# Weight pieces and two first layers kept in order, state products on the mix's PSUM buffers, a sorting copy moved

## The chip, the cores and the metric

The kernel runs on one core of a Trainium2 chip. The metric is the device time of one execution in microseconds; less is better. The core has five engines with a queue of instructions each: PE (matrix products, into the eight banks of PSUM), DVE and ACT (element-wise work, and all reading of PSUM), POOL (element-wise work in SBUF and indirect DMAs) and SP (here only DMA issues). Every engine works through its own queue in order and waits on semaphores for the others.

## What is computed

A block-wise linear attention with decay, then a Fourier mixing block with a two-layer network:

```python
for b in range(nb):                      # attention, blocks of 64 rows
    intra = einsum('bhic,bhjc->bhij', qb, kb) * Dmask
    intra = einsum('bhij,bhjd->bhid', intra, vb)
    inter = einsum('bhid,bhde->bhie', qb * lam_pow, kv_state)
    out[:, :, sl] = intra + inter
    kv_state = lam_block * kv_state + einsum('bhsd,bhse->bhde', kb * rev_pow, vb)
x = out as (B, S, H*D)
u = x + real(fft(fft(x, axis=1), axis=2))
un = (u - mean(u)) / sqrt(var(u) + 1e-6)
return u + maximum(un @ w_ch1, 0) @ w_ch2
```

Batch 4, 8 heads of 64, 768 rows, width 512, hidden width 2048. All products are in f32. The two weight matrices come as f64 and are turned into f32 on the chip with bit operations.

## The kernel before

**Attention** (`attention`, line 526) is a generator of twelve steps: four batches, three steps each, 256 rows a step. It yields an estimate of time at three places of a step, and a planner mixes other work in there. In step i: `turn_k` and `turn_q` transpose the next step's k and q on PE into PSUM, and ACT copies them out (L391 to L398); DVE multiplies q by its powers of the decay, `qpow` (L400). `sort` (L380) is a POOL copy of k for the step after that, which waits for the load of k. `back` transposes the outputs of the step before into rows (L467; DVE L490 and L491 or ACT L474 to L478 copy them out). `to_state` multiplies k and v (L406) into PSUM; DVE adds the product to the state (L414, L416), and POOL makes the next decayed state (`decayed`, L421). `within` makes the outputs (L447). Then the loads of later steps are issued on SP (L367, L371). `begin` makes the scores (L426, DVE L432 multiplies by the decays), scales k on POOL (L386) and adds the state's part (L441).

**PSUM.** While `strict[0]` holds, tiles are taken from eight fixed banks by hand: `psum_t` goes round banks 0 to 3 (transposes, scores, state products), `psum_o` round 4 and 5, and `psum_a` round 6 and 7 (everything of the mix). Later, tiles come from two pools of five and three buffers.

**The mix** (`fft_ln`, line 698) of one batch: DVE folds the rows (L597 to L691), PE makes five products with the Fourier tables (L724, ACT L728), then three wide products (L736 to L741, DVE L816 to L831), statistics on DVE (L755, L756) and POOL (L759, L760), and for three pairs of row tiles a norm (`norm`: DVE L776, and where the first network takes them PE transposes L783 and ACT L787). For batch 0 the last two norms are not run there but put into `held`, and the network's generator calls them later.

**Weights** (`weights`, line 274): 32 pieces of 128x512. The first sixteen are the first half of both matrices. Each is fetched (`fetch`) and converted (`convert`): DVE L261, ACT L262, DVE L263, L266, L269, L270, one unit of the planner's time. While `strict[0]` holds, the fetch goes through ACT's queue into buffers of the network, up to two pieces ahead; later through SP's queue into the three `words` buffers, which attention also uses for k and q.

**The network** (`mlp`, line 871): for 256 rows a first layer (L878, ACT L886 or DVE L884) and a second layer (L892). Each product in f32 stands in the trace as two matmul records, so half a first layer (eight column blocks of four products) is 64 records of L878.

**Order.** `P(i)` keeps an instruction in program order among all that are kept, as long as `strict[0]` holds; `keep` does so always. Everything else is placed by the scheduler of the language, which may put it ahead of kept instructions on the same engine. The driver (lines 1516 to 1542) writes the mixing out: `mixed((gen, t), ...)` advances that generator which has used the smallest share of its t; `run` exhausts one. It starts with attention alone, mixes in weight pieces until the first batch's rows are there, then the mix of batch 0, attention and pieces in four stages, then what is left of attention, then pieces until eight have landed. There `strict[0]` ends. The first layers of the first two networks follow beside pieces, and then the rest: network halves beside the mixes of batches 1 to 3 and the remaining pieces. From L1160 on come the last row tiles with a seven-product scheme, which the change does not touch.

Of the kernel before, what the change touches and what calls it, by code (L numbers as in the profile page):

```python
# [11 lines left out]
F32 = mybir.dt.float32  # L12
# [65 lines left out]
def kernel(  # L78
# [69 lines left out]
    def P(i):  # L148
        return keep(i) if strict[0] else i
# [5 lines left out]
    banks = [new(pa, [128, 512], "pa") for _ in range(5)] + [new(pm, [128, 512], "pm") for _ in range(3)]  # L155
    turn = {"s": 0, "m": 0, "o": 0}

    def held_bank(i, shape):
        t = banks[i]
        if len(shape) == 2:  # L160
            return t[:, 0:shape[1]]
        return t[:, 0:shape[1] * shape[2]].rearrange("p (a b) -> p a b", a=shape[1])
# [9 lines left out]
    def psum_a(shape):  # L172
        if strict[0]:
            turn["m"] += 1
            return held_bank(6 + turn["m"] % 2, shape)
        return new(pa, shape, "pa")
# [15 lines left out]
    for hd in HD:  # L192
        P(nc.vector.tensor_copy(pulse[hd, 1:C + 1:2], ident[hd, hd]))
    decay = const.tile([128, H, C + 1], F32, name="decay")
    for h in [*range(0, H, 2), *range(1, H, 2)]:
        P(scan(decay[:, h, :], lamb[:, h:h + 1].broadcast_to([128, C + 1]), pulse, 0.0, op0=ALU.mult, op1=ALU.add))

    lamq = const.tile([128, HP], F32, name="lamq")
# [4 lines left out]
    for m in [1 << e for e in range(7)]:  # L203
        P(nc.vector.tensor_tensor(qpow[:, :, m:2 * m], qpow[:, :, 0:m], qpow[:, :, m - 1:m].broadcast_to([128, HP, m]), op=ALU.mult))
    spow = qpow[:, :, C - 1:C]

# [23 lines left out]
    def load_tables(i):  # L230
        if i == 1:
            P(nc.sync.dma_start(cs, cn["cs"].ap()))
            P(nc.sync.dma_start(ix, cn["ix"].ap()))
        elif i == 2:
            P(nc.sync.dma_start(dt, cn["dt"].ap()))
# [5 lines left out]
    def fetch(j, src):  # L241

        if strict[0]:
            raw = hp_.tile([128, 2 * WP], U32, tag="hr", name=f"raw{j}")
        else:
            raw = words[j % 3].bitcast(U32)
        if strict[0]:
            P(nc.scalar.dma_start(raw, src.bitcast(U32)))
        else:
            P(nc.sync.dma_start(raw, src.bitcast(U32)))  # L250
        return raw
# [150 lines left out]
    def to_state(i):  # L402
        n, vt, kd = i % SC, v_of[i % 2], k_of[i % 2]
        chunks = (0, 1) if n < SC - 1 else (0,)
        pu = [psum_t([128, HP, D]) for _ in chunks]
        lead(P(mm(pu[ch][HD[hi], hp, :], lhsT=kd[HD[ch], 2 * hp + hi, r, :], rhs=vt[HD[ch], 2 * hp + hi, r, :],  # L406
# [119 lines left out]
    def attention():  # L526
# [26 lines left out]
        for i in range(n):  # L553
            yield 1.5
            if i + 1 < n:
                turn_k(i + 1)
                if i + 2 < n:
                    sort(i + 2)
                turn_q(i + 1)
            yield 2.5  # L560
            if i:
                back(i - 1)
            if i + 1 < n:
                to_state(i + 1)
            within(i)
            if i + 2 < n:
                load(i + 2, "v")
            if i + 3 < n:
                load(i + 3, "kq")
            if i in TABLES:  # L570
                load_tables(TABLES[i])
            yield 5.0
            if i + 1 < n:
                begin(i + 1)
# [8 lines left out]
    odd = const.tile([128, HM], F32, name="bs")  # L583
    for t in ys + [odd]:
        P(nc.gpsimd.memset(t, 0.0))

# [111 lines left out]
    def fft_ln(b):  # L698
# [104 lines left out]
        def wide(t):  # L803
            ps = psum_a([128, DM])
            width(t, ps, False, keep if (b, t) == PLAIN[1] else lambda i: i)
            A = halves(ps)[:, ::-1, 0:QM]
# [6 lines left out]
        def summed(t, ds, A):  # L813
            if strict[0]:
                yield 0.6
            P(nc.vector.tensor_tensor(even_odd(ds[:, 0:HM]), A, even_odd(odd[:, :]), op=ALU.subtract))  # L816
            P(nc.vector.tensor_tensor(even_odd(ds[:, HM + 1:2 * HM + 1]), A, even_odd(odd[:, :]), op=ALU.add))
            u, v_ = xs[b, t], xs[b, HC + t]
            if strict[0]:
# [29 lines left out]
        if b in LEADS:  # L849
            two, none = norm(2), norm(0)  # L850
            held.update({(b, 1, 1): two, (b, 1, 4): two, (b, 1, 7): none, (b, 1, FO): none})
            return
# [626 lines left out]
    def run(gen):  # L1479
        return sum(gen)  # L1480
# [37 lines left out]
    run(part(att, 9.0))  # L1518
    run(mixed((until(att, lambda: (0, 0) in xs), 20.0), (w, 4.0)))
    run(mixed((mix, T_FOLD), (att, 3.6 * t_step)))  # L1520
    run(mixed((mix, 8.0), (att, 0.9 * t_step), (w, 2.5)))
    run(mixed((mix, 22.0), (att, 3.0 * t_step), (w, 1.0)))
    run(mix)
# [5 lines left out]
    lead_half = chain(half[0])  # L1529
    run(mixed((att, 1.3 * t_step), (w, 1.5)))  # L1530
    run(att)
    run(until(w, lambda: landed[0] >= 8))
    strict[0] = False
    run(mixed((part(lead_half, 13.5), 13.6), (w, 2.0)))
    run(mixed((part(half[0][1], 13.5), 13.6), (w, NW / 2 - landed[0])))
    run(until(w, lambda: landed[0] >= NW // 2))
    run(mixed((lead_half, t_half - 27.0), (fr, 62.0), (w, 0.5 * NW)))
    run(w)
# [49 lines left out]
```

## Time and profile before

| | us |
|---|---|
| median of 3 runs | 792.33 |
| lowest, highest | 791.04, 792.41 |
| the profiled execution | 791.95 |
| its span, first to last instruction | 790.1 |
| PE busy | 748.2 (95%) |
| DVE busy | 612.6 (78%) |
| ACT busy | 200.5 (25%) |
| POOL busy | 184.7 (23%) |

A row of a timeline has the start, the busy time, engine, line, operation, what is written from what, the shape and the count; in brackets stands the idle time of the engine just before it and who ended it. A row of the groups has the busy time and the mean of one in ns, then the idle time before them. Times are from the span's start. A PE that is busy need not be at its peak, and the granted clock is given as a share of full speed.

### The profile page before, as it was taken

What the parts mean: (1) busy time and instruction counts of PE and PEld (TensorE: products, weight loads), DVE (VectorE), ACT (ScalarE), POOL (GpSimd) and SP (SyncE); (2) the same over time, 40 slices, a digit from 0 to 9 for tenths busy, and PEclk for the clock granted to TensorE, in tenths of its full rate; (3) what the DMA queues carried; (4) which work ended last, traced back from release to release, by engine and by line L of the source; (5) the groups of instructions that cost most, each with busy time, mean ns of one, the idle gap of its engine ahead of it and who ended that gap; (6) DMA issues with size and microseconds to landing.
All of it is one profiled execution on the core that took longest, in us unless ns stands there. A gap on an engine that the chain in (4) does not pass through costs nothing.

```text
span 790.1 us, 17058 instructions
## 1 busy us (share of the span) xinstructions
PE 748.2 (95%) x6872; PEld 650.6 (82%) x6872; DVE 612.6 (78%) x1183; ACT 200.5 (25%) x468; POOL 184.7 (23%) x215
## 2 busy tenths in 40 slices
PE   6879995989999999999899999999999999999997
PEld 5758895878567749568755889999999999999997
DVE  6758865786998848754894899878997599758983
ACT  2344453343233112001100221023410342024310
POOL 4323433120001114210101980460014100230013
PEclk9989999889999999999999999999999999999999
DMA  9759888244253345730341365777544456355441
GB/s 210 233 155 236 230 222 260 92 147 147 93 161 100 87 126 182 159 107 27 74 109 58 135 200 162 253 246 230 149 162 150 148 187 184 122 185 176 134 147 67
DMA packets 132739, 123.49 MB, mean 156 GB/s; under 512 B 67006, under 2 KB 93246, under 8 KB 132662
## 3 DMA queue, kind: packets, MB, share of 16 engines
q1 hardware_dynamic: 126470, 102.09, 45.1%
q0 software_dynamic: 4032, 12.99, 4.7%
q10 hardware_dynamic: 2160, 7.35, 2.7%
q8 instruction: 54, 0.88, 0.5%
q14 instruction: 23, 0.19, 0.1%
HBM read 90.66 MB, written 31.73 MB: 155 GB/s over the span
## 4 chain that ended last, share of the span: by engine, by line
PE 78%; DVE 9%; DMA 5%; issue 4%; ACT 2%; POOL 1%; SPq 0%; ACTq 0%; DVEq 0%; POOLq 0%
PE p L1327 19%; PE p L1253 17%; PE pm L878 11%; PE pm L892 10%; PE p L1160 5%; PE pa L724 3%; PE pa L426 2%; PE pm L447 1%; PE pa L406 1%; PE pa L397 1%; PE pa L447 1%; PE pa L467 1%; PE pa L391 1%; DVE stt L755 1%; PE pm L724 1%
## 5 line engine op out<-in xcount | busy, mean ns | idle before, releaser
L878 PE MATMUL pm<-ut,w 128*128 128x256 f32 x512 | 115.6, 381 | 2.6 <-DVE hr L884 1.5
L878 PEld LDWEIGHTS pm<-ut,w 128*128 128x128 f32 x512 | 96.3, 190 | 19.8 <-issue 3.7
L892 PE MATMUL pm<-w,hr 128*128 128x512 f32 x240 | 104.8, 592 | 0.0
L892 PEld LDWEIGHTS pm<-w,hr 128*128 128x128 f32 x240 | 45.2, 190 | 52.9 <-issue 52.6
L1348 POOL TENSOR_TENSOR y<-y,u 128x512 f32<-128x512 f32 x12 | 19.9, 1659 | 186.5 <-DVE y L1357 155.2
L1327 PE MATMUL p<-tx,sx 128*128 128x128 f32 x400 | 52.7, 275 | 0.0
L1327 PEld LDWEIGHTS p<-tx,sx 128*128 128x128 f32 x400 | 48.6, 192 | 0.0
L1262 DVE TENSOR_TENSOR ha<-p,ha 128x512 f32<-128x512 f32 x60 | 40.0, 683 | 8.3 <-PE p L1253 8.2
L886 ACT ACTIVATE hr<-pm 128x256 f32<-128x256 f32 x44 | 16.8, 381 | 95.3 <-PE pm L878 95.2
L1333 ACT COPY y<-p 128x128 f32<-128x128 f32 x48 | 12.7, 265 | 103.6 <-PE p L1327 103.2
L262 ACT ACTIVATE e<-e,cvt 128x512 uint16<-128x512 uint16 x32 | 23.1, 726 | 59.1 <-DVE e L261 56.5
L1335 DVE TENSOR_TENSOR y<-p,y 128x128 f32<-128x128 f32 x92 | 25.5, 284 | 16.1 <-PE p L1327 9.4
L1327 PE MATMUL p<-w,ha 128*128 128x128 f32 x288 | 37.4, 275 | 0.0
L1262 DVE TENSOR_TENSOR hs<-p,hs 128x512 f32<-128x512 f32 x39 | 26.1, 683 | 12.3 <-PE p L1253 12.3
L1327 PEld LDWEIGHTS p<-w,ha 128*128 128x128 f32 x288 | 34.9, 192 | 0.1
L1253 PE MATMUL p<-sx,tx 128*128 128x128 f32 x264 | 33.9, 275 | 0.0
L426 PE MATMUL pa<-w 64*64 64x128 f32 x768 | 30.1, 295 | 3.6 <-issue 2.1
L1253 PEld LDWEIGHTS p<-sx,tx 128*128 128x128 f32 x264 | 31.6, 192 | 0.0
L426 PEld LDWEIGHTS pa<-w 64*64 64x64 f32 x768 | 26.0, 147 | 6.4 <-issue 3.3
L867 POOL DMA_INDIRECT out_dram<-y,ix x12 | 13.5, 1126 | 75.8 <-DVE y L927 64.0
L1253 PE MATMUL p<-ur,w 128*128 128x128 f32 x216 | 28.0, 275 | 0.0
L776 DVE TENSOR_SCALAR un<-x,mv,rs 128x256 f32<-128x256 f32 x44 | 16.2, 406 | 14.5 <-POOL rs L760 8.4
(327 smaller groups left out, 1896.6 us busy)
## 6 DMA issues: line engine op xcount, KB each, us to landing
tx<-td SPq DMA_DIRECT2D x84, 256.0 KB, 2.9
tx<-sd SPq DMA_DIRECT2D x63, 256.0 KB, 2.9
words<-in_moe_w_ch_dram SPq DMA_DIRECT2D x20, 512.0 KB, 3.9
w<-in_v_dram SPq DMA_DIRECT2D x12, 512.0 KB, 5.8
raw<-in_moe_w_ch_dram ACTq DMA_DIRECT2D x12, 512.0 KB, 7.3
words<-in_k_dram SPq DMA_DIRECT2D x11, 512.0 KB, 7.0
td<-tx SPq DMA_DIRECT2D x21, 256.0 KB, 2.0
ud<-x SPq DMA_DIRECT2D x16, 256.0 KB, 2.3
```

The lines of the kernel that those rows point to most:

```text
L262: P(nc.scalar.activation(pw, pw, AF.Relu, bias=cvt[:, 0:1], scale=8.0))
L426: lead(P(mm(pss[r][hi][HD[ch], hp, :], lhsT=kT[HD[hi], r, hp, D * ch:D * ch + D], rhs=qT[HD[hi], hp, C * ch:C * ch + C], start=True, stop= ...
L724: mm = P(nc.tensor.matmul(ps[:, n, :], lhsT=piece(a, i, n), rhs=cs[0:rows, a, i in (2, 3), n, :], start=(a == 0), stop=(a == 1)))
L878: P(nc.tensor.matmul(ps, lhsT=w1[:, c, 128 * fc:128 * fc + 128], rhs=ut[:, c, :], start=(c == 0), stop=(c == KO - 1)))
L886: P(nc.scalar.activation(t, ps, AF.Relu))
L892: return P(nc.tensor.matmul(ps, lhsT=hr[(fc - f0) // 4][:, fc % 4, 128 * i:128 * i + 128], rhs=w2[:, fc, :], start=(fc == f0), stop=(fc == ...
L1160: nc.tensor.matmul(ps, lhsT=s2.A[a][:, kt, 128 * i:128 * i + 128], rhs=U[b][:, kt, :], start=(first and kt == 0), stop=(kt == 1), skip_gro ...
L1253: nc.tensor.matmul(ps[:, 128 * i:128 * i + 128], lhsT=ab[m][0][:, 128 * i:128 * i + 128], rhs=ab[m][1], start=(start and i == 0), stop=Tru ...
L1262: V.tensor_tensor(o, p, o, op=ADD)
L1327: nc.tensor.matmul(ps[:, 0:HM // 2], lhsT=ab[m][0][i], rhs=ab[m][1][:, i, :], start=(start and i == 0), stop=(i == HF // 2 - 1), skip_grou ...
L1335: V.tensor_tensor(o, ps[:, 0:HM // 2], o, op=ADD)
L1348: nc.gpsimd.tensor_tensor(o, y, u, op=ADD)
```

## The change

- The first sixteen weight pieces and the first layers of the first two networks are kept in program order: `strict[0]` now ends when sixteen pieces have landed, behind those two first layers. A new flag `over`, set when attention has ended, takes over the choice of the fetch's queue and buffers, and from then `psum_a` goes round all eight banks (`rest`).
- State products take the mix's banks 6 and 7 from the third step on, except while a wide product of the mix has been made and not yet read (`unread`).
- `sort` comes behind `to_state`, and so behind its `decayed`, on POOL.
- The query powers are made ahead of the decay scans; six memsets of the mix's buffers move from the start to the third step.
- The two held norms of batch 0 run in the mix itself, with a wait of 1.5 units between.
- Attention's yields are 3.0, 2.0 and 4.0 in place of 1.5, 2.5 and 5.0. The shares of weight pieces in the five mixed stages are 2.0, 1.4, 1.6, 3.0 and 2.0 in place of 4.0, 0, 2.5, 1.0 and 1.5, and 3.0 in place of 2.0 beside the first of the two first layers.

```diff
+    rest, unread, over = [6, 7], [False], [False]
...
-            return held_bank(6 + turn["m"] % 2, shape)
+            return held_bank(rest[turn["m"] % len(rest)], shape)
...
-    decay = const.tile([128, H, C + 1], F32, name="decay")
-    for h in [*range(0, H, 2), *range(1, H, 2)]:
-        P(scan(decay[:, h, :], lamb[:, h:h + 1].broadcast_to([128, C + 1]), pulse, 0.0, op0=ALU.mult, op1=ALU.add))
...
     for m in [1 << e for e in range(7)]:
         P(nc.vector.tensor_tensor(qpow[:, :, m:2 * m], qpow[:, :, 0:m], qpow[:, :, m - 1:m].broadcast_to([128, HP, m]), op=ALU.mult))
+    decay = const.tile([128, H, C + 1], F32, name="decay")
+    for h in [*range(0, H, 2), *range(1, H, 2)]:
+        P(scan(decay[:, h, :], lamb[:, h:h + 1].broadcast_to([128, C + 1]), pulse, 0.0, op0=ALU.mult, op1=ALU.add))
...
         if i == 1:
+            for t in ys + [odd]:
+                P(nc.gpsimd.memset(t, 0.0))
...
-        if strict[0]:
+        if not over[0]:
             raw = hp_.tile([128, 2 * WP], U32, tag="hr", name=f"raw{j}")
         else:
             raw = words[j % 3].bitcast(U32)
-        if strict[0]:
+        if not over[0]:
             P(nc.scalar.dma_start(raw, src.bitcast(U32)))
...
-        pu = [psum_t([128, HP, D]) for _ in chunks]
+        pu = [(psum_t if unread[0] or i < 2 else psum_a)([128, HP, D]) for _ in chunks]
...
-            yield 1.5
+            yield 3.0
             if i + 1 < n:
                 turn_k(i + 1)
-                if i + 2 < n:
-                    sort(i + 2)
                 turn_q(i + 1)
-            yield 2.5
+            yield 2.0
             if i:
                 back(i - 1)
             if i + 1 < n:
                 to_state(i + 1)
+            if i + 2 < n:
+                sort(i + 2)
             within(i)
...
-            yield 5.0
+            yield 4.0
...
-    for t in ys + [odd]:
-        P(nc.gpsimd.memset(t, 0.0))
...
             ps = psum_a([128, DM])
+            unread[0] = True
...
             P(nc.vector.tensor_tensor(even_odd(ds[:, HM + 1:2 * HM + 1]), A, even_odd(odd[:, :]), op=ALU.add))
+            unread[0] = False
...
-            two, none = norm(2), norm(0)
-            held.update({(b, 1, 1): two, (b, 1, 4): two, (b, 1, 7): none, (b, 1, FO): none})
+            yield from norm(2)
+            yield 1.5
+            yield from norm(0)
             return
...
-    run(mixed((until(att, lambda: (0, 0) in xs), 20.0), (w, 4.0)))
-    run(mixed((mix, T_FOLD), (att, 3.6 * t_step)))
-    run(mixed((mix, 8.0), (att, 0.9 * t_step), (w, 2.5)))
-    run(mixed((mix, 22.0), (att, 3.0 * t_step), (w, 1.0)))
+    run(mixed((until(att, lambda: (0, 0) in xs), 20.0), (w, 2.0)))
+    run(mixed((mix, T_FOLD), (att, 3.6 * t_step), (w, 1.4)))
+    run(mixed((mix, 8.0), (att, 0.9 * t_step), (w, 1.6)))
+    run(mixed((mix, 30.0), (att, 3.2 * t_step), (w, 3.0)))
     run(mix)
...
-    run(mixed((att, 1.3 * t_step), (w, 1.5)))
+    run(mixed((att, 1.2 * t_step), (w, 2.0)))
     run(att)
-    run(until(w, lambda: landed[0] >= 8))
-    strict[0] = False
-    run(mixed((part(lead_half, 13.5), 13.6), (w, 2.0)))
+    over[0] = True
+    rest[:] = [0, 1, 2, 3, 4, 5, 6, 7]
+    run(mixed((part(lead_half, 13.5), 13.6), (w, 3.0)))
     run(mixed((part(half[0][1], 13.5), 13.6), (w, NW / 2 - landed[0])))
     run(until(w, lambda: landed[0] >= NW // 2))
+    strict[0] = False
     run(mixed((lead_half, t_half - 27.0), (fr, 62.0), (w, 0.5 * NW)))
```

## The prediction

> **What bounds the kernel now.** I read the page first: the span and the slices of PE, which show gaps in the first fifth and hardly any behind it. Then I cut the span into stages with the table by stage, and in each stage asked the timelines of PE, DVE, POOL and SP what ended the idle time.
>
> ```profile
> span 790.1 us, 17058 instructions
> ...
> 10.26:27.00 16.74, 14.60 (x382) 13.71 (x383) 8.74 (x16) 4.17 (x9) 8.22 (x10) 1.00 0.88 213
> 27.00:62.00 35.00, 27.35 (x486) 23.96 (x485) 24.26 (x47) 14.44 (x31) 8.72 (x10) 0.90 0.75 203
> 62.00:98.80 36.80, 34.21 (x933) 30.77 (x932) 31.01 (x62) 16.50 (x42) 14.71 (x16) 1.00 0.86 231
> 98.80:124.00 25.20, 23.77 (x484) 22.19 (x483) 17.98 (x35) 13.06 (x31) 8.18 (x10) 1.00 0.82 218
> 124.00:168.80 44.80, 32.15 (x593) 28.79 (x590) 31.39 (x65) 14.40 (x37) 12.91 (x16) 0.85 0.50 148
> 168.80:292.00 123.20, 123.08 (x483) 85.38 (x483) 96.54 (x212) 33.98 (x76) 9.09 (x12) 1.00 0.44 132
> ```
>
> The columns of the table are the stretch, its length, busy time of PE, of its weight loads, of DVE, ACT and POOL, the granted clock, the DMA share and GB/s. From 168.8 on PE is full (123.08 of 123.2 us). Attention and the first mix end at 168.8. Before that PE stands idle in three places: a little at the start, 7.65 us in 27 to 62, and 12.65 us in 124 to 168.8. Only there can an edit of queues win time; what follows 168.8 is nearly the same work and starts earlier if these shrink. The same two long stages have a clock below 1.00. Cut finer, it was at 0.50 in four stretches:
>
> ```profile
> 48.05:51.46 3.41, 3.41 (x98) 3.41 (x91) 1.57 (x5) 0.00 (x0) 0.62 (x1) 0.50 0.02 5
> 58.29:61.70 3.41, 3.41 (x18) 3.32 (x17) 2.23 (x5) 1.59 (x4) 2.06 (x3) 0.50 1.28 262
> 136.80:143.62 6.82, 4.97 (x68) 4.60 (x72) 5.54 (x12) 1.17 (x2) 1.14 (x2) 0.50 0.34 104
> 160.69:167.52 6.83, 6.19 (x74) 5.36 (x74) 6.64 (x13) 2.31 (x7) 1.69 (x3) 0.50 0.33 115
> ```
>
> Each begins in or right behind idle time of PE. At half clock PE work takes twice its time, so half of the busy time is lost: 1.7, 1.7, 2.5 and 3.1 us. These are the gaps that stand before them, PE's rows first, then SP's and DVE's:
>
> ```profile
> 23.96 0.99 PE L426 MATMUL pa<-w 64*64 64x128 f32 x27 [1.41 <-DVE st L416]
> 38.57 1.16 PE L391 MATMUL pa<-ident,w 128*128 128x128 f32 x8 [0.94 <-DVE w L432]
> 42.18 1.14 PE L467 MATMUL pa<-ident,oT 128*128 128x128 f32 x8 [1.25 <-ACT w L392]
> 47.00 0.33 PE L406 MATMUL pa<-w,words 64*64 64x64 f32 x4 [1.98 <-issue]
> 56.68 1.16 PE L391 MATMUL pa<-ident,w 128*128 128x128 f32 x8 [1.76 <-DVE w L432]
> 129.24 1.16 PE L406 MATMUL pa<-w,words 64*64 64x64 f32 x64 [1.57 <-DMA w<-in_v_dram]
> 138.65 1.11 PE L783 MATMUL pm<-ident,un 128*128 128x128 f32 x4 [6.51 <-DVE un L776]
> 161.33 1.97 PE L467 MATMUL pa<-ident,oT 128*128 128x128 f32 x8 [4.57 <-DVE w L432]
> ...
> 129.03 1.60 SPq L250 DMA_DIRECT2D words<-in_moe_w_ch_dram  x1
> ...
> 135.98 0.43 DVE L263 TENSOR_SCALAR w<-words 128x512 uint32<-128x512 uint32 x1 [7.38 <-DMA words<-in_moe_w_ch_dram]
> 136.32 0.41 DVE L416 TENSOR_TENSOR st<-st,pa 128x256 f32<-128x256 f32 x1
> ```
>
> The largest gap is told by the last three rows. A weight piece that is not pinned, fetched only at 129.03, was placed on DVE ahead of the pinned state sum of L416. DVE stood 7.38 us for its DMA, and the state, the norm and PE stood with it.
>
> **The change part by part.** *The sorting copy behind the decay.* In the first step POOL's order costs this:
>
> ```profile
> 21.83 1.04 POOL L380 COPY w<-words 128x1024 f32<-128x1024 f32 x1 [2.96 <-DMA words<-in_k_dram]
> 22.83 0.61 POOL L421 TENSOR_TENSOR st<-st,qpow 128x256 f32<-128x256 f32 x1
> ...
> 23.48 0.42 DVE L416 TENSOR_TENSOR st<-st,pa 128x256 f32<-128x256 f32 x1 [2.86 <-POOL st L421]
> ```
>
> DVE's wait of 2.86 began at 20.6, when its first sum was done. The decay L421 could run then, and stood behind a copy that waits for k. Reversed, it ends at 21.3 and the second L416 comes 2.1 us sooner; PE gets back its 1.41. The copy still ends at 22.9. Later copies now stand behind DVE's sum, and the scale of L386 behind them; POOL is busy 8.7 of 35 us in the next stage, which covers that. −1.4, between 0 and −2.1.
>
> *Query powers first, memsets later.* Same instructions; the scans come some us later on DVE, but PE's first products wait for q and not for them. The six memsets go to POOL after the third step, where it is mostly idle. 0, within 0.5 either way.
>
> *Weight pieces.* One costs DVE the sum of these means, 3.1 us:
>
> ```profile
> L266 DVE SCALAR_TENSOR_TENSOR w<-raw,w 128x512 f32<-128x512 uint32 x11 | 8.9, 814 | 0.2
> L269 DVE SCALAR_TENSOR_TENSOR e<-raw,e 128x512 uint16<-128x512 uint16 x10 | 6.9, 687 | 4.6 <-ACT e L262 4.6
> L270 DVE SCALAR_TENSOR_TENSOR w<-w,e 128x512 f32<-128x512 f32 x9 | 6.2, 692 | 0.3
> L261 DVE TENSOR_SCALAR e<-raw 128x512 uint16<-128x512 uint16 x11 | 5.3, 483 | 0.6 <-DMA raw<-in_moe_w_ch_dram 0.6
> L263 DVE TENSOR_SCALAR w<-raw 128x512 uint32<-128x512 uint32 x11 | 4.6, 415 | 0.0
> ```
>
> In 27 to 62 the quota falls from four to two. The gaps at 38.57, 42.18 and 56.68 (3.95 us) stand behind a piece's DVE or ACT work; two of three go, −2.6. *State products on the mix's banks*: the gap of 1.98 at 47.00 is the state product waiting for buffers that DVE was still reading, and DVE then waits in its turn:
>
> ```profile
> 49.12 0.42 DVE L414 COPY st<-pa 128x256 f32<-128x256 f32 x1 [1.56 <-PE pa L406]
> 49.62 0.62 POOL L421 TENSOR_TENSOR st<-st,qpow 128x256 f32<-128x256 f32 x1 [5.91 <-DVE st L414]
> 50.28 0.42 DVE L416 TENSOR_TENSOR st<-st,pa 128x256 f32<-128x256 f32 x1 [0.73 <-POOL st L421]
> ```
>
> With other banks the product runs beside DVE's copies and 1.5 of the 1.56 goes. Of the two half-clock stretches here I count one as gone, −1.7. Together −5.8; from −2 (one gap) to −9 (all gaps and both stretches).
>
> A rule bears on this last term. The Trainium skill (TensorE: Matmul & The Clock Gate, Part 1) says that PE falls to half clock after an idle window of about 3.4 us. The trace differs: the gaps ahead of 48.05 and 58.29 are 1.98 and 1.76 us, so here shorter idle time was enough. By the page's rule as it stands neither stretch would come from these gaps, and the sum would be 1.7 us smaller.
>
> In 62 to 98.8 some one and a half pieces come where none was: 4.7 us of DVE into 36.8 − 31.0 = 5.8 free us, with PE at 34.2. That is tight: +1.0, between 0 and +4.7; the state products' small waits there return 0.7. Net +0.3. In 98.8 to 124 PE has 1.4 us to give and loses one piece's company: 0.
>
> *All sixteen pieces pinned.* The converts can no longer stand ahead of attention's last steps. The state product at 129.24 ends at 130.40, so L416 starts there and not at 136.32: −5.9, and the half-clock stretch behind the gap goes too, −2.5. What is late next is DVE itself. Its busy time in 124 to 168.8 was 31.4, about four pieces' worth in it:
>
> ```profile
> L266 DVE SCALAR_TENSOR_TENSOR w<-raw,w 128x512 f32<-128x512 uint32 x4 | 3.5, 869 | 0.1
> L266 DVE SCALAR_TENSOR_TENSOR w<-words,w 128x512 f32<-128x512 uint32 x3 | 2.1, 690 | 0.1
> L270 DVE SCALAR_TENSOR_TENSOR w<-w,e 128x512 f32<-128x512 f32 x2 | 1.4, 691 | 0.1
> ```
>
> Seven were half done and two finished. After, two of the last stage's three pieces and two more behind it fall there: about the same. But the two held norms come in, of which six L776 were still to run:
>
> ```profile
> L776 DVE TENSOR_SCALAR un<-x,mv,rs 128x256 f32<-128x256 f32 x4 | 1.5, 410 | 0.8 <-POOL rs L760 0.8
> ...
> 171.82 0.44 PE pa L783 x4
> ...
> 332.04 13.81 PE pm L878 x64
> ```
>
> Six at 0.41 are 2.5 us, so DVE needs 33.9, and 44.8 − 8.4 = 36.4 leaves it 2.5 us for its hops to POOL and PE. I therefore count nothing for the gap of 4.57 and the last half-clock stretch. −8.4; −3 if the pieces block the steps in order, −11 if DVE runs without a break.
>
> *Norms moved, two first layers pinned.* Four transposes of 0.44 us leave a stage where PE is full: −1.8. The two pinned first layers are 27.6 us of PE (13.81 each); the six pieces left are 18.6 us of DVE beside them. 0, up to +3 if relus on ACT queue behind the pieces' ACT step.
>
> Sum: −1.4 − 5.8 + 0.3 − 8.4 − 1.8 = −17.1. The profiled execution took 791.95 us, 1.85 over its span and 0.38 under the median of 792.33. 792.33 − 17.1 = 775.2.
>
> **The rivals.** *The pieces come back in order.* Pinned pieces stand in DVE's queue where the scheduler had chosen free places, and the last stage is DVE's. For it: 31.4 of 44.8 busy and every gap on PE there ended by DVE. Against it: total DVE work before 168.8 hardly grows. Then the tail gives −3, the first stage −3, the folds +2, the rest −3: 785.
>
> *The hoisting stays.* Work of the next mix is still free to move, and SP or DVE could again stop at a DMA: the load of v at 129.24 was late by 1.57. Without the −8.4: 784. Against it: pieces after the sixteenth need buffers that pinned pieces free.
>
> *Given back later.* DVE is busy 96.5 of 123.2 us behind 168.8; if the next mix's loads do not move forward with PE's work, PE meets the gap there. Up to all of it: 791.
>
> *Shared banks stall PE (the slower side).* Ten steps put one or two state products on two banks that the mix also uses. A product of the mix behind them waits until L414, L421 and L416 are through, 1.6 us by the rows at 49.12 to 50.70, and a state product behind the mix waits for an ACT copy, about 0.6. PE runs in order, so all behind stands. Both in all ten steps would be +22: 797. It decides from 1.9 us a step on. Against it: the state goes elsewhere while a wide product is unread, and attention's own products of L447 follow each state product ahead of the mix's. The Trainium skill (TensorE: Matmul & The Clock Gate, A second HAM failure mode) speaks for it: it tells of short idles from cycling through PSUM banks that drop the clock. In this trace the mix cycled through two banks in 62 to 124 at clock 1.00.
>
> **How the numbers follow.** Forecast 0.55; pieces in order 0.18; hoisting stays 0.08; given back 0.10; shared banks 0.09. The range takes the forecast's bounds down to 766 (the tail at −11, the first stage at −9) and reaches over the first two rivals to 787. About 0.2%, 1.6 us, is what a measurement of this kernel tells from no change. Given back splits between a small gain and none: faster 0.84, same 0.07, slower 0.09.
>
> **What would show it.** Right: no DVE wait for `words` while L416 is pending; no wait for k ahead of the first step's L421; no stretch at 0.50 near 137; the last attention transposes at about 153; PE full from there to 405. Wrong: L406 or L724 waiting for L416 or ACT copies in every step; DVE waits on ACT in front of L432 in the last three steps; a new gap of PE between the first layers and 300.

## The result and the profile after

| | before | after |
|---|---|---|
| median of 6 runs, us | 792.15 | 787.23 |
| lowest, highest | 787.45, 793.53 | 785.20, 788.46 |
| the profiled execution | 791.95 | 785.49 |
| its span | 790.1 | 783.6 |

The ratio is 0.9942, with an interval of 0.9914 to 0.9971. The change makes the kernel 4.9 us faster; I had forecast 17.1. From the ends of the interval the gain is between 2.3 and 6.8 us, so the difference from the forecast is no matter of noise.

The same table by stage, of the kernel after, with the same cuts until 124; attention and the first mix now end at 162.5. The last two rows are the only stretches at half clock while PE had work (it falls once more when PE is done, at the span's end).

```profile
27.00:62.00 35.00, 31.31 (x747) 27.93 (x746) 29.00 (x54) 18.70 (x45) 15.64 (x20) 1.00 0.91 237
62.00:98.80 36.80, 33.49 (x803) 30.64 (x800) 33.28 (x63) 16.92 (x41) 13.02 (x14) 1.00 0.86 232
98.80:124.00 25.20, 19.43 (x371) 17.53 (x370) 15.21 (x29) 9.90 (x22) 10.63 (x11) 0.93 0.81 216
124.00:162.50 38.50, 28.05 (x576) 24.69 (x576) 27.55 (x60) 15.59 (x38) 10.09 (x11) 0.91 0.32 101
162.50:292.00 129.50, 126.96 (x496) 88.81 (x495) 105.79 (x232) 32.85 (x77) 11.23 (x13) 1.00 0.45 137
...
120.64:124.05 3.41, 3.40 (x17) 3.00 (x15) 0.20 (x1) 2.35 (x4) 0.00 (x0) 0.50 0.31 60
...
141.12:147.94 6.82, 4.12 (x18) 3.71 (x19) 3.04 (x9) 1.93 (x4) 1.64 (x3) 0.50 0.00 0
```

The first stretch holds far more work than before (747 matmul records for 486) at full clock: there the change did what it should. From 98.8 on it is PE that has room: 5.8 of 25.2 us idle where it was 1.4, and 10.5 of 38.5 in the last stage. The two longest idle times in PE's timeline of the kernel after, and one of 1.73 us, are all at the same line, L784, the norm's transposes (L783 before; most lines have moved by one to four, and are named here by what they do). Those at 119.92 and 125.77 belong to norm 1, which ran in the mix before the change too; the one at 143.31 belongs to norm 2, one of the two that the change moves:

```profile
119.92 0.76 PE L784 MATMUL pm<-ident,un 128*128 128x128 f32 x4 [3.69 <-DVE un L777]
...
125.77 0.76 PE L784 MATMUL pm<-ident,e 128*128 128x128 f32 x4 [1.73 <-DVE e L777]
...
143.31 1.09 PE L784 MATMUL pm<-ident,un 128*128 128x128 f32 x4 [7.00 <-DVE un L777]
144.91 1.11 PE L784 MATMUL pm<-ident,un 128*128 128x128 f32 x4 [0.51 <-DVE un L777]
145.82 1.92 PE L394 MATMUL pa<-ident,w 128*128 128x128 f32 x8
```

The 7.00 us are the largest, and what stands behind them matters most: L394 is `turn_k` of attention's last step, an operation that needs nothing of the norm. Its input, the copy of k on POOL, was finished at 131.82:

```profile
130.78 1.04 POOL L383 COPY w<-words 128x1024 f32<-128x1024 f32 x1
```

It also needs a PSUM buffer from which DVE still reads step 10's scores. In e1 (below), where no norm stands ahead of it, it runs 0.83 us after that reading begins, which would be 138.3 here (an estimate); it ran at 145.82.

DVE's timeline shows what PE waits for. Up to the norm it never stops; it works through a chain at whose end the norm L777 stands: the rest of the wide sums (L818 to L825), the scores of step 10 (L435), the edge rows (L831 to L834), a weight piece (L269), the statistics, and then the norm.

```profile
135.47 0.42 DVE L818 TENSOR_TENSOR ds<-pm,bs 128x256 f32<-128x256 f32 x1
...
136.86 0.68 DVE L825 TENSOR_TENSOR x<-x,ds 128x512 f32<-128x512 f32 x1
137.47 0.69 DVE L435 TENSOR_TENSOR w<-pa,decay 128x512 f32<-128x512 f32 x1
...
140.59 0.67 DVE L269 SCALAR_TENSOR_TENSOR w<-raw,w 128x512 f32<-128x512 uint32 x1
141.19 0.67 DVE L756 BATCH_NORM_STATS2 stt<-x 128x6 f32<-128x512 f32 x1
...
142.69 0.18 DVE L757 BATCH_NORM_AGGREGATE mv<-stt 128x2 f32<-128x6 f32 x1
142.79 0.71 DVE L777 TENSOR_SCALAR un<-x,mv,rs 128x256 f32<-128x256 f32 x2
144.44 0.73 DVE L777 TENSOR_SCALAR un<-x,mv,rs 128x256 f32<-128x256 f32 x2 [0.95 <-PE pm L784]
148.98 1.29 DVE L403 TENSOR_TENSOR w<-pa,qpow 128x512 f32<-128x512 f32 x2 [3.80 <-ACT w L401]
```

So the wait for `words` that I had read as the worst thing in the kernel before is gone, and in its place stands another wait on the same engine at nearly the same point: 7.00 us for 6.51, and again followed by 6.8 us at half clock. The Trainium skill (TensorE: Matmul & The Clock Gate, Part 1) says that PE falls to half clock after an idle window of about 3.4 us. The trace agrees here: the gap began at 136.3 and the clock was at 0.50 from 141.12.

Where in the span the time came and went is best seen by attention's steps. This table has, from the timelines, the start of the first score multiplication on DVE of steps 3, 7, 8, 10 and 11 (counted from 0), and the end of attention (its last transposes on PE). The last two columns are worked out: the time from step 8's mark to the end of attention, and from there to the span's end. It includes the kernels tried, which are explained below.

| kernel | 3 | 7 | 8 | 10 | 11 | end | 8 to end | behind |
|---|---|---|---|---|---|---|---|---|
| before | 55.9 | 96.4 | 110.3 | 142.7 | 160.6 | 168.8 | 58.5 | 621.3 |
| after | 46.6 | 86.8 | 104.4 | 137.5 | 156.3 | 162.5 | 58.1 | 621.1 |
| e1 norms held | 47.1 | 87.8 | 105.3 | 140.1 | 150.5 | 156.6 | 51.3 | 625.3 |
| e4 pin alone | 53.9 | 94.0 | 107.6 | 133.0 | 146.9 | 153.2 | 45.6 | 626.0 |
| e6 pin, banks | 51.2 | 91.4 | 105.0 | 132.0 | 146.0 | 152.3 | 47.3 | 624.8 |
| e9 held, paced | 46.1 | 86.3 | 103.8 | 127.9 | 142.6 | 150.9 | 47.1 | 628.3 |
| e10 norms in the mix | 51.5 | 92.5 | 106.8 | 134.1 | 154.3 | 163.4 | 56.6 | 624.6 |

By step 7 the kernel after is 9.6 us ahead of before. Of that it has 5.9 left at step 8, because more of the mix's products fall between these two marks (17.6 us in place of 13.9, with PE busy for 17.28 of them). From step 8 to the end, where the pinned pieces should have saved most, it saves 0.4. Behind the end of attention the two are alike. The question for the experiments is therefore why pinning the pieces saves nothing there.

### The profile page after: what moved, and what is told of

Its sections match the earlier page's. It is cut to its first block, busy times and chain, and to the rows that moved or that the text cites. A ratio compares the mean times of both kernels' runs of the same rounds, so it can differ in the third digit from the quotient of the medians.

```text
span 783.6 us, 17057 instructions
## 1 busy us (share of the span) xinstructions
PE 742.9 (95%) x6872; PEld 645.0 (82%) x6872; DVE 612.8 (78%) x1183; ACT 200.9 (26%) x468; POOL 189.3 (24%) x215
## 4 chain that ended last, share of the span: by engine, by line
PE 68%; DVE 17%; issue 7%; DMA 4%; POOL 3%; ACT 1%; SPq 0%; DVEq 0%; POOLq 0%; ACTq 0%
PE p L1331 21%; PE p L1257 17%; PE pm L896 7%; PE pm L882 7%; PE p L1164 5%; PE pa L882 2%; PE pa L725 2%; DVE w L273 1%; DVE e L272 1%; DVE w L269 1%; DVE stt L756 1%; PE pa L450 1%; PE pa L429 1%; DMA w<-in_v_dram 1%; PE pm L725 1%
## 5 line engine op out<-in xcount | busy, mean ns | idle before, releaser
L882 PE MATMUL pm<-ut,w 128*128 128x256 f32 x432 | 97.7, 380 | 3.2 <-DVE hr L888 1.5
L882 PEld LDWEIGHTS pm<-ut,w 128*128 128x128 f32 x432 | 81.2, 190 | 18.1 <-issue 3.3
L890 ACT ACTIVATE hr<-pm 128x256 f32<-128x256 f32 x34 | 13.0, 381 | 84.3 <-PE pm L882 83.4
L1257 PE MATMUL p<-sx,tx 128*128 128x128 f32 x264 | 33.9, 275 | 0.0
L871 POOL DMA_INDIRECT out_dram<-y,ix x12 | 13.6, 1130 | 76.0 <-DVE y L931 64.3
L429 PE MATMUL pa<-w 64*64 64x128 f32 x768 | 27.4, 277 | 3.9 <-issue 2.0
L429 PEld LDWEIGHTS pa<-w 64*64 64x64 f32 x768 | 23.5, 136 | 6.3 <-issue 3.2
L612 POOL DMA_INDIRECT fo<-xa,ix x6 | 7.1, 1182 | 86.3 <-PE pa L725 74.0
```

The lines of the kernel that those rows point to most:

```text
L429: lead(P(mm(pss[r][hi][HD[ch], hp, :], lhsT=kT[HD[hi], r, hp, D * ch:D * ch + D], rhs=qT[HD[hi], hp, C * ch:C * ch + C], start=True, stop= ...
L871: P(nc.gpsimd.indirect_dma_start(out=out_high, out_offset=row_of(2 + HC * (b + 1) + T - HC), in_=y[:, :], in_offset=None))
L882: P(nc.tensor.matmul(ps, lhsT=w1[:, c, 128 * fc:128 * fc + 128], rhs=ut[:, c, :], start=(c == 0), stop=(c == KO - 1)))
L1257: nc.tensor.matmul(ps[:, 128 * i:128 * i + 128], lhsT=ab[m][0][:, 128 * i:128 * i + 128], rhs=ab[m][1], start=(start and i == 0), stop=Tru ...
```

## The experiments

The theory: the norms 2 and 0, now run in the mix and in order, put transposes that wait for DVE's chain into PE's queue ahead of attention's last steps, and this takes what the pinned pieces give. The rivals: the three weight pieces in the last mixed stage fill DVE, which then is the limit whatever PE's order; pinning the pieces isn't worth what I forecast; the shared banks, the new shares or the moved copy cost something that the trace does not show plainly. Each ratio is against the kernel before, run beside it on the same chip; the medians of before were 789.69 to 791.71 us in those, so kernels are compared by their ratios, with the two intervals' half widths added as squares, and 1% taken as 7.9 us.

**The norms held, fewer pieces, both** (each against the kernel after).

```diff
-                if plain and strict[0]:
+                if plain and strict[0] and g == 1:
...
-            yield from norm(2)
-            yield 1.5
-            yield from norm(0)
+            two, none = norm(2), norm(0)
+            held.update({(b, 1, 1): two, (b, 1, 4): two, (b, 1, 7): none, (b, 1, FO): none})
```

> The kernel after, with the norms 2 and 0 of batch 0 held for the network again; all else as after. Theory N (a new wait took the place of the old one: kept in program order inside the mix, the norms' transposes L784 stand in PE's queue ahead of attention's last steps, and PE waits 7.0 us for DVE's L777 and runs 6.8 us at half clock behind it): the gap of 7.0 and the half-clock stretch behind it go, 6 to 9 us under the kernel after, about 779 us, ratio to before 0.981 to 0.986. Theory D (DVE is the bound of the last steps, whatever PE's order): the gap moves to the products behind DVE's score multiplications, and the time stays within 2 us of the kernel after, 785 to 789.

The second kernel changes only one share:

```diff
-    run(mixed((mix, 30.0), (att, 3.2 * t_step), (w, 3.0)))
+    run(mixed((mix, 30.0), (att, 3.2 * t_step), (w, 1.0)))
```

> The kernel after, with one weight piece in place of three beside the last two wide products of the first mix (share 1.0 in place of 3.0); the pieces follow beside the first layers. Theory D: two pieces of 3.1 us leave DVE's queue ahead of the norm and the scores, 4 to 6 us under the kernel after, about 782. Theory N: the transposes wait for DVE's wide sums and statistics, of which none goes; 0 to 2 us under the kernel after, 785 to 787. If the first layers cannot hide eight pieces (24.8 us of DVE in 27.6), up to 3 us is lost again.

The third has both edits:

> Norms held and one piece, both edits at once. Theory N: as with the norms held alone, about 779, the second edit within 2 us. Theory D: as with one piece alone, 782. If both hold, they add: 774 to 777.

Measured: e1 784.38 us, ratio 0.991 (0.9883 to 0.9936); e2 786.95, 0.9937 (0.9913 to 0.9961); e3 787.84, 0.9968 (0.9948 to 0.9988). Fewer pieces alone show no gain (0.4 ± 2.9 us against the kernel after, which had 0.9942), so the pieces of the last stage are not the cause. With the norms held, attention ends at 156.6 for 162.5 in the profiled execution, and the 7.00 us are gone, but only 1.7 us of that reached the span, and between the ratios of e1 and of the kernel after there is 2.5 ± 3.1 us: by itself no proof, and nearer to the rival's size than to the theory's. Two things in the profile of e1 say why it is so small. Step 10's mark is even later (140.1), since norm 1 and both sets of wide products still crowd into the step before it; and norm 1's transposes, which stay in the mix, make PE wait just as they do in the kernel after. Behind that wait stands a long stretch at half clock, in which 7.61 us of PE's work were done:

```profile
120.82 1.12 PE L784 MATMUL pm<-ident,un 128*128 128x128 f32 x4 [3.69 <-DVE un L777]
...
119.90:130.15 10.25, 7.61 (x35) 7.15 (x36) 4.50 (x9) 3.52 (x6) 0.71 (x1) 0.50 0.35 68
```

And behind the end of attention 4.2 us are lost again. e3 came out as none of its expectations had it: against e1, the two pieces taken out cost 4.6 ± 2.6 us. Its attention ends at 156.8, like that of e1; its loss lies behind, where the profile has 628.8 us. I saw a wait of 2.23 us for the next mix's folds and a clock of 0.86 in 280 to 292 there, and did not follow it further.

**The pin alone, and one part at a time on top of it.** The fourth kernel is the kernel before with only the sixteen pieces and the two first layers pinned, and what belongs to that (the flag `over`, and all eight banks for `psum_a` once attention has ended); norms 2 and 0 stay held.

```diff
-        if strict[0]:
+        if not over[0]:
...
-                if plain and strict[0]:
+                if plain and strict[0] and g == 1:
...
-    run(until(w, lambda: landed[0] >= 8))
-    strict[0] = False
+    over[0] = True
+    rest[:] = [0, 1, 2, 3, 4, 5, 6, 7]
...
     run(until(w, lambda: landed[0] >= NW // 2))
+    strict[0] = False
```

> The kernel before with one edit alone: the sixteen pieces and the two first layers kept in order (strict ends behind them; fetches of later pieces on SP as soon as attention has ended). The prediction's step: DVE's wait of 7.4 us for the words and the half-clock stretch behind it go, 8.4 us under the kernel before, 783 to 785. Rival (the norm's transposes wait for DVE in any case, since its L776 stand behind the scores): PE's gap at L783 shrinks only to 3 to 4 us, 3 to 5 us under before, 787 to 789.

Measured: 782.92 us, ratio 0.99 (0.9874 to 0.9927), 8.0 us faster than before (5.8 to 10.0 by the interval). I had forecast 8.4 for this part. The pin alone is faster than the whole change (by 3.3 ± 3.1 us from the ratios). This is the timeline of DVE at the place where it had stood 7.38 us for `words`:

```profile
127.40 0.42 DVE L417 TENSOR_TENSOR st<-st,pa 128x256 f32<-128x256 f32 x1 [1.32 <-PE pa L407]
129.65 0.42 DVE L417 TENSOR_TENSOR st<-st,pa 128x256 f32<-128x256 f32 x1 [1.83 <-POOL st L422]
129.99 0.73 DVE L777 TENSOR_SCALAR un<-x,mv,rs 128x256 f32<-128x256 f32 x2
130.63 0.73 DVE L777 TENSOR_SCALAR e<-x,mv,rs 128x256 f32<-128x256 f32 x2
...
133.01 0.69 DVE L433 TENSOR_TENSOR w<-pa,decay 128x512 f32<-128x512 f32 x1 [0.32 <-PE pa L427]
```

The state sums wait only for their product and for POOL, and norm 1 follows at once. From step 8 to the end it takes 45.6 us for 58.5. Of the 15.6 us by which attention ends earlier, 4.7 are given back behind it. These rows are the stretches before and behind the end of attention, first of the kernel before and then of this one; PE busy grows by 2.0 us and its idle time by 2.7:

```profile
168.80:790.10 621.30, 611.18 (x3986) 528.00 (x3985) 490.88 (x943) 134.31 (x316) 127.14 (x140) 1.00 0.47 145
```

```profile
0.00:153.20 153.20, 128.40 (x2885) 113.38 (x2886) 116.62 (x229) 66.18 (x153) 56.06 (x74) 1.00 0.79 206
153.20:779.20 626.00, 613.18 (x3988) 528.12 (x3987) 495.23 (x955) 134.55 (x316) 132.35 (x141) 1.00 0.48 147
```

On this kernel one part each of the rest of the change, first the shares of the pieces (2.0, 1.4, 1.6, 2.0 and 2.0 in the five stages):

> The sixteen pieces pinned as in the run with that edit alone (782.9 us there), and the shares of weight pieces 2.0, 1.4, 1.6, 2.0 and 2.0 in place of 4.0, 0, 2.5, 1.0 and 1.5 (nine pieces as before; a piece less beside the last wide products than in the kernel after). The prediction's step: two of three gaps go in the first steps, step 4 begins 3 to 4 us earlier, 779 to 780 us. Rival (what leaves the first steps comes back later, since DVE's work is the same): step 4 is earlier but attention's end is not, 782 to 784.

then the state products on the mix's banks (`unread` and the choice in `to_state`, as in the change):

> The sixteen pieces pinned, and the state products on the mix's two banks except while a wide product is unread. The prediction's step: PE's waits at the state product (7.2 us in the run with the pin alone, by L407) fall under 2 us and 1.5 to 2.2 us are won, 781 us. Rival (shared banks stall PE): new waits of PE at the Fourier products or the state products, 784 or more.

then the sorting copy behind the decay:

> The sixteen pieces pinned, and the sorting copy behind the state's decay. The prediction's step: the second step's scores 1.4 to 2.1 us earlier, and 1.4 us at the end, 781.5 us. Rival (a later wait takes it up): the scores of the second step earlier, but no more than 0.5 us at attention's end, 782.5 to 783.5.

and the three together, with the yields of before:

> The pin, the shares, the banks and the sorting copy together, with the kernel before's yields, the norms held and the mix at the pace before. If the three add up: attention's step 7 some 7 us earlier than with the pin alone (the kernel after has it 7.2 us earlier), attention's end at 146, and 775 to 777 us. If the last steps or what follows attention take it back: step 7 as early, and 780 to 783.

| | us | ratio | interval | against the pin alone, us |
|---|---|---|---|---|
| e5 shares | 779.85 | 0.9852 | 0.9828 to 0.9876 | −3.8 ± 2.8 |
| e6 banks | 777.88 | 0.9831 | 0.9805 to 0.9857 | −5.5 ± 2.9 |
| e7 copy | 782.28 | 0.9898 | 0.9862 to 0.9935 | −0.2 ± 3.6 |
| e8 all three | 779.16 | 0.984 | 0.9814 to 0.9867 | −4.7 ± 3.0 |

None of the three shows a cost. The banks gain more than I forecast for them, the shares about as much; whether the three add up these four kernels cannot tell (9.5 us singly and 4.7 together differ by 4.8 ± 6.2; e12 below tells more). e6 has the lowest time of the study and beats both kernels: 13.8 us under before. The decay's wait behind the copy went as I said. This is POOL in the first step of e7, where the decay no longer stands behind the copy that waits for k:

```profile
19.53 0.62 POOL L422 TENSOR_TENSOR st<-st,qpow 128x256 f32<-128x256 f32 x1 [2.11 <-DVE st L417]
21.53 1.04 POOL L381 COPY w<-words 128x1024 f32<-128x1024 f32 x1 [1.38 <-DMA words<-in_k_dram]
```

Counted as in the table, the scores of step 1 come at 21.6 for 23.5 in e4, yet those of step 2 at 36.9 for 37.5, and those of step 3 are later, at 54.9 for 53.9. One profile on each side is all I have for that, and in that of e7 the clock fell to 0.50 at 46.8 and again at 56.9, where e4's stayed at 1.00.

**Norms held and the mix at its old pace.** In e1 the last mixed stage still ran the mix at 30 units over 3.2 steps of attention. This kernel is e1 with the pace of before and two pieces:

```diff
-    run(mixed((mix, 30.0), (att, 3.2 * t_step), (w, 3.0)))
+    run(mixed((mix, 22.0), (att, 3.0 * t_step), (w, 2.0)))
```

> The kernel after with the norms held, and the last mixed stage at the pace of the kernel before (mix 22.0 over three steps in place of 30.0 over 3.2; two pieces in place of three). Theory P (after the norms, what is left of the loss is the mix's pace: both remaining wide products, the first norm and the pieces fall into step 9 to 10, which takes 23.3 us against 11 to 12 in the runs with the pin alone): step 9 to 10 falls under 14 us, attention ends at 150 to 153, 777 to 780 us. Rival Y (attention's new yields or the order at the start do it): step 9 to 10 stays above 18, 783 to 785.

Measured: 782.21 us, ratio 0.9883 (0.9862 to 0.9904), 4.7 ± 2.8 us faster than the kernel after. The time is above the 777 to 780 expected; the marks are as expected. The step from mark 9 to mark 10 takes 13.6 us where e1 took 23.3 (and the kernel after 21.6). Norm 1's transposes make PE wait 1.15 us there, for 3.69 in e1, and the clock is full:

```profile
114.30:127.90 13.60, 10.42 (x220) 8.47 (x222) 10.21 (x20) 6.49 (x16) 5.09 (x6) 1.00 0.88 233
```

**The norms put into the mix of the best version.** This is the disputed step alone: e6 with the two norms in the mix, and with the stage's numbers raised so that mix and attention keep their rates (7.4 units a step for 7.3):

```diff
-                if plain and strict[0] and g == 1:
+                if plain and strict[0]:
...
-            two, none = norm(2), norm(0)
-            held.update({(b, 1, 1): two, (b, 1, 4): two, (b, 1, 7): none, (b, 1, FO): none})
+            yield from norm(2)
+            yield 1.5
+            yield from norm(0)
...
-    run(mixed((mix, 22.0), (att, 3.0 * t_step), (w, 1.0)))
+    run(mixed((mix, 27.0), (att, 3.65 * t_step), (w, 1.0)))
```

> The pin and the banks (777.9 us), and the two norms in the mix as in the kernel after, at an unchanged pace of the mix. Theory N (the norms' transposes in PE's order make PE wait for DVE): a gap of 3 to 7 us at L784 in the last two steps, attention's end 3 to 7 us later, 781 to 784 us. If the norms cost nothing by themselves and only the pace does: 777 to 779.

Measured: 788.16 us, ratio 0.9956 (0.9936 to 0.9975): 9.9 ± 2.6 us slower than e6, and above the 781 to 784 us expected. The step itself, which I had put at −1.8, costs ten on this kernel. PE's timeline of e10 repeats that of the kernel after:

```profile
149.97 1.09 PE L784 MATMUL pm<-ident,un 128*128 128x128 f32 x4 [5.40 <-DVE un L777]
150.99 0.47 PE L442 MATMUL pa<-w,st 64*64 64x128 f32 x2
...
152.75 2.33 PE L427 MATMUL pa<-w 64*64 64x128 f32 x64
157.13 0.76 PE L784 MATMUL pm<-ident,un 128*128 128x128 f32 x4 [2.05 <-DVE un L777]
```

Behind the wait of 5.40 us stand the state's part (L442) and the scores (L427) of attention's last step, and they run at once when the transposes are through. DVE in its turn then stands for those scores:

```profile
149.44 0.70 DVE L777 TENSOR_SCALAR un<-x,mv,rs 128x256 f32<-128x256 f32 x2
154.27 0.69 DVE L433 TENSOR_TENSOR w<-pa,decay 128x512 f32<-128x512 f32 x1 [4.12 <-PE pa L427]
```

The table by stage has the same work from step 10's mark to step 11's, first in e6 and then in e10, and for e10 the stretch at half clock that begins in the gap:

```profile
132.00:146.00 14.00, 13.61 (x306) 12.55 (x298) 11.82 (x26) 5.34 (x16) 3.58 (x5) 1.00 0.26 84
```

```profile
134.00:154.40 20.40, 15.00 (x298) 14.00 (x294) 13.95 (x31) 5.92 (x17) 5.71 (x8) 0.83 0.14 46
...
146.80:153.60 6.80, 3.63 (x52) 3.33 (x56) 3.17 (x10) 0.59 (x1) 2.12 (x3) 0.50 0.12 31
```

About as many matmuls (306 and 298), 6.4 us more. In the two profiles attention ends 11.1 us later in e10. Of these, 9.0 lie behind step 10's mark, where the moved norms stand; 2.1 lie before it, where e10 has one more stretch at half clock (at 116.1, behind the shared banks' wait told below), and are not the norms'. Behind attention the two are alike. So on this kernel the theory holds: the move makes PE wait in order, and that costs far more than the transposes.

**Two tries to go on from e6.** In e6 the shared banks do stall PE, once:

```profile
114.31 1.09 PE L407 MATMUL pm<-w,words 64*64 64x64 f32 x58 [2.15 <-DVE ds L819]
```

The flag `unread` is cleared before DVE has read the wide product, in program order before the yield of 1.6 in `summed`. One kernel clears it behind that yield, so that this state product goes to other banks:

> The pin and the banks, and a wide product's bank counted as unread until the next place where attention may come in. In the run with pin and banks PE waited 2.15 us at a state product for DVE's L819, the one place where a shared bank stalled it. If that wait is on the path: it goes, 775.5 to 777 us. If DVE is late there in any case: the wait moves to the scores, 777 to 779.

Measured: 780.12 us, ratio 0.9863 (0.9836 to 0.989). The wait is gone and attention ends at 149.8 for 152.3, but the time isn't better than that of e6; with 2.5 ± 3.0 us against it the two are not told apart. The other adds the shares of e5 to e6:

> The pin, the banks and the shares of pieces 2.0, 1.4, 1.6, 2.0 and 2.0, without the sorting copy's move. Alone on the pin, the banks gave 5 us and the shares 3. If they add up: 774 to 776 us, attention's end at 149 to 150. If both won the same waits of the first steps, or the last steps are bound by DVE's whole work whatever came before: attention's end at 151 to 153, and 777 to 780, as with the sorting copy too.

Measured: 778.4 us, ratio 0.986 (0.9837 to 0.9882). Again attention ends earlier (151.0), and again the kernel is no faster than e6 (2.3 ± 2.7 us against it). Singly on the pin, banks and shares gave 5.5 and 3.8 us; together they give 3.2, which is 6.1 ± 3.9 less than their sum. So these two gains do not add. Among e5, e6, e8, e11 and e12 step 7's mark and the end of attention vary, with ratios of 0.9831 to 0.9863: what one of them wins early is not seen at the end of the span. What takes it up I did not isolate.

## Why the prediction was wrong

The predicted direction held; the size did not. By its steps:

*The sorting copy*, −1.4: the wait left the first step as described, and 0.2 ± 3.6 reached the time (e7). The forecast lies inside that, so the time neither shows nor refutes it.

*The first stage*, −5.8: right in place, too small in size. At step 3 the kernel after is 9.3 us ahead of before, where the copy and this term together gave 7.2. Measured each by itself on the pin, the shared banks are worth 5.5 us and the shares 3.8; I had 1.5 for the banks (the one gap of 1.98 us that I saw), and 4.3 for two of the three gaps and a half-clock stretch. The folds' +0.3 cannot be told from this. The gap of 1.98 us at the state product is gone in e6. What I did not see is that these gains don't add: banks and shares together are worth 3.2 (e12), and with the copy's move 4.7 (e8).

*All sixteen pieces pinned*, −8.4: the mechanism was right. DVE's wait for `words` and the stretch at half clock behind it are gone in e4. That the size agrees too, with −8.0, is in part luck: from step 8 to the end of attention e4 takes 12.9 us less, since PE's gap of 4.57 us shrinks to 1.06 and the last half-clock stretch goes, for which I had counted nothing; and 4.7 us are given back behind, for which I had counted nothing either.

*Norms moved, two first layers pinned*, −1.8: **this is the step that failed.** I priced the move by the work that it shifts: four transposes of 0.44 us leave a stage where PE is full, and DVE has room for the rest, since 33.9 us of work are less than the 36.4 that remain. Both are sums of busy time. What the move does is put an instruction that waits into a queue that runs in order: L784 ahead of attention's last step, at the end of a serial chain on DVE. I had written that 2.5 us were left "for its hops to POOL and PE". What this leaves out is the order: in the kernel after, PE stands 7.00 us while DVE works without a break, and DVE then stands 3.80 us for the copy of the query transposes, which PE could run only behind the norm's. The experiment that makes this move on e6 measures +9.9 ± 2.6. On the kernel after, undoing it alone gives 2.5 ± 3.1 (e1), and with the mix's pace 4.7 ± 2.8 (e9); how much of that is the norms' and how much the pace's these runs do not separate. In the kernel before, the held norms were called by the network later, and their transposes, at 171.66 to 200.58, ran between first layers without a wait of PE.

How the forecast of −17.1 becomes what was measured (−4.6 by the ratio) can be worked out from the ratios, each difference with some 3 us of uncertainty. Without the norms' term the forecast is −15.3; the kernel that comes nearest to it, e8, gives −12.6: 2.7 us too many, for parts that do not add. From e8 to e9 3.4 ± 2.7 us are lost with what else differs (the yields, the query powers and memsets, the shares beside attention's end and the first layer); I tried none of these by itself, so that stays open. From e9 to the kernel after come 4.7 ± 2.8, by the two norms and the mix's faster pace, where I had −1.8: 6.5. Together, before rounding, these are the 12.5 us that were missing. The range's lower bound of 766 is an error of its own: with the tail at −11 and the first stage at −9, which are named for it, the sum gives 769.4.

*The signs named.* No wait for `words` with L416 pending, and no wait for k ahead of the first step's decay: both held. The end of attention, "about 153", is 162.5 in the kernel after and 153.2 in e4, which has the pin without the norms; and instead of none there is a stretch at 0.50 from 141.12. From the end of attention to 405 PE is idle for 5.0 us, before for 4.1, so there is no new gap of any size.

*The rivals.* The shared banks (797 us) were wrong: they gain. A wait of PE at them does occur, but as 2.15 us at one place of e6, where I had allowed for two in each of ten steps. The Trainium skill (TensorE: Matmul & The Clock Gate, A second HAM failure mode) tells of short idles from cycling through PSUM banks that drop the clock. Here it came up in some runs: behind the same wait for a shared bank, 2.04 us in e8 and 2.14 us in e10, the clock was at 0.50 from 114.1 and from 116.1, for 3.4 us each; in e6, behind 2.15 us, it stayed at 1.00. The prediction's own reading, that the mix had cycled through two banks at full clock from 62 on, holds for a shorter time than it says, since the mix's first products (L724) run from 99.6 on in the kernel before. "The hoisting stays" was wrong (e4). "Given back later" is part of the truth, though not for the kernel after, which has 621.1 us behind attention as before has 621.3: in the kernels that end attention ten or more us sooner, 3.5 us (e6) to 8.6 us (e8) are given back; e8's profiled execution was its slowest, 5.6 us above its median. "The pieces come back in order" came nearest in its mechanism: something pinned does block the steps in order. It was the norms, not the pieces: fewer pieces showed no gain.

## What to carry to other kernels

An instruction that is moved in an in-order queue is not priced by its own length but by how long it will stand there waiting, and by what of the queue behind it could have run; before the move, look up the chain that produces its input on the other engine, and find the end of that chain in time, not its busy sum. In the last stage here PE and DVE fed each other in small steps; each was idle for more than a quarter of it in the kernel after, and yet there was no free room for a third party's work in the same order. When several edits of such a stage each gain, time the combination too: here the pin with one further edit (777.9 us) could not be told from the pin with two or three.

## What the runs showed of the chip that I had not expected

The granted clock fell for about 3.41 us or a multiple of that: the stretches at 0.50 lasted 3.41 and 6.82 us in the kernels before and after, about 6.8 in e10 and 10.25 in e1. They lie on a fixed raster. Cut the kernel before into cells of 3.413 us, at 48.05 and on both sides of it, from 17.3 to the end of attention: PE was busy 34%, 48%, 0% and 0% of the cells just ahead of the four stretches, and at least 54% of every other cell at full clock. Only the span's first cell, without any PE work, is out of line: no stretch followed it. So what counts here is not one long gap but the idle time of a cell taken together, and the limit is near half of it; in other kernels a cell with 58% was still followed by a stretch (e8, the cell up to 148.2), and one with 43% was not (e10, up to 157.0). This is why the short gaps ahead of 48.05 and 58.29 (the longest 1.98 and 1.76 us) were enough, and why the wait at the shared banks dropped the clock in e8 and e10 (40% and 37% busy) and not in e6 (55%): it depends on where in the raster a gap falls. The executions of one kernel seem to differ by how many such stretches they catch. The profiled ones of e4 and e11 had a mean clock of 1.000, and their times of 781.02 and 777.13 us were each the lowest of their kernel; the runs of e4 with 0.991 and 0.992 took 786.00 and 784.06. One stretch of 6.8 us with PE busy costs half of that, so a single profiled execution of this kernel is good to about 3 us (an estimate), which is as much as most of the parts weighed here.
